# Starting the first FFN block in halves, separate PSUM tiles for the q and k transposes, and x of two groups transposed by DMA, in a fused chunk-attention and FFN kernel

## The chip, the cores and the metric

The kernel runs on one core of a Trainium2 chip. TensorE multiplies matrices and writes to PSUM tiles; VectorE, ScalarE and GpSimd copy, cast and work element by element; SyncE issues DMA transfers. The granted clock is the share of TensorE's full speed that the profile shows as granted: 1.00 is full, 0.50 is half. The metric is the device time of one execution in microseconds (us). Most executions of one kernel agree within a per cent or so; a run that is over 1.5% above the fastest of the same kernel on its chip is called slow and is left out of comparisons. Ratios below are the mean time of one kernel's fast runs over the mean of the other's fast runs in the same rounds on the same chip, so they are not quite the ratio of the medians that are quoted beside them. The kernel before alone had medians of 298 to 301 us on the chips used here, so times from different chips are not compared to less than a per cent.

## The reference, cut to what matters

```python
# q, k, v: (8 batches, 8 heads, 576 positions, 64), float32; attention inside chunks of 64 positions
scores = scale * q_c @ k_c.T            # per chunk
attn   = softmax(scores)
x      = (attn @ v_c) -> (4608 tokens, 512)
out    = relu(x @ w_in)**2 @ w_out      # w_in (512, 2048), w_out (2048, 512)
```

The 4,608 tokens are 18 groups of 256. Two groups make an FFN block of 512 tokens, nine blocks in all (0 to 8).

## The kernel before

TensorE runs the FFN of one block while the attention of the next block is slipped in between, at numbered slots: one slot per `ft` (one of 16 column tiles of `w_in`) of the first FFN matmul, then one per quarter of an output tile of the second. For groups 0 to 3, q and k are transposed on TensorE; from group 4 on they are loaded, cast to bf16 by GpSimd (`C`) and transposed by DMA (`TD`). x is transposed on TensorE below group `FIRST_DMA_X` and by DMA from there on. SyncE issues the loads and the transposes in program order; where an instruction waits, those behind it wait too.

```python
FIRST_DMA_T = 4
FIRST_DMA_X = 6
ps_ffn = tile_pool(name="ps_ffn", bufs=4, PSUM)      # tiles of 128 x 512 fp32
ps_att = tile_pool(name="ps_att", bufs=2, PSUM)      # tiles of 128 x 1024 fp32

def transpose_qk(g):
    ps = ps_att.tile([128, 1024], FP32, name="ps_att").bitcast(BF16)   # q and k in one tile
    ...
    for which in range(2):
        transpose_paired(g, which, ps[:, which * 1024:(which + 1) * 1024])
    for which, copy in enumerate((nc.vector.tensor_copy, nc.scalar.copy)):
        copy_paired(copy, qkT[:, which], ps[:, which * 1024:(which + 1) * 1024])

# ... the start: filler matmuls (keep_busy) between the pieces of the first attention
XE(0); keep_busy(8); AV(1); keep_busy(8)
transpose_x_early(1, 0); keep_busy(4); transpose_x_early(1, 1); keep_busy(4)

# ... the plan by slots; SC = scores, AV = values, XT = transpose of x
if j == 0:
    for slot, f in ((24, T), (27, SC), (29, AV), (31, XT)):
        at(slot, f, nxt[0])
    at(31, T, nxt[1])
    phases = [ffn_in(0, 0, 512), ffn_out_by_ft(0)]
elif j == 1:
    go_slots = [*range(17), *range(34, 48)]           # one load issued in each of these slots
    loads = itertools.chain(pieces(nxt), *map(qk_pieces, far))
    ...
    for i, g in enumerate(nxt):
        for slot, f in ((22 + 4 * i, C), (27 + 4 * i, TD), (37, SC), (39 + 2 * i, AV), (42 + 2 * i, XT)):
            at(slot, f, g)
else:
    slots = {SC: 8, AV: 11, XT: 15, C: 14, TD: 19}
    if j == 2:
        slots = {SC: 6, AV: 11, XT: 14, C: 20, TD: 24}
    ...
# at the end of block 1: C and TD of groups 6 and 7
```

In block 1 `nxt` is groups 4 and 5 and `far` is groups 6 and 7. The loads of q and k of 6 and 7 go out in slots 34 to 43, their casts and transposes at the end of the block, and their scores stand in slot 6 of block 2.

The softmax here doesn't subtract the row's maximum and nothing guards it: scores larger than these inputs give would overflow.

## Time and profile before

| | before |
|---|---|
| median of the first three runs | 298.04 us (296.81 to 302.14) |
| profiled execution | span 294.9 us, granted clock 1.00 |
| TensorE busy | 282.1 us, 96% |
| start of the first FFN matmul of block 1 / second of block 1 / first of block 2 / first of block 3 | 52.60 / 70.27 / 86.86 / 116.28 us |

The main lines of this profile stand in the prediction below. Four more are SyncE's issues of the last loads and transposes ahead of block 2's scores (start, duration, line, what):

```profile
77.55 0.83 SPq L110 DMA_DIRECT2D k_sb<-in_k_dram  x1
...
80.44 2.97 SPq L110 DMA_DIRECT2D q_sb<-in_q_dram  x1
83.46 0.91 SPq L110 DMA_DIRECT2D k_sb<-in_k_dram  x1
84.55 6.57 SPq L223 DMA_TRANSPOSE qkT<-qkb  x2
```

The two transposes of q and k follow the last load. The second of them lands at 93.3 us (issued 89.40, 3.9 us), where the scores of groups 6 and 7 run (93.06 to 93.76).

### The profile page before, as it was taken

How to read it: one execution, taken by the hardware profiler on the slowest of the kernel's cores; microseconds unless marked ns; L12 is line 12 of the kernel's file. 1: busy time of each engine (PE TensorE's matmuls, PEld its weight loads, DVE VectorE, ACT ScalarE, POOL GpSimd, SP SyncE). 2: the span in 40 equal slices, each digit the busy share in tenths (PEclk: the TensorE clock that was granted, in tenths of full speed). 3: DMA queues.
4: the chain of work that ended last, by engine and by line, in shares of the span. 5: the costliest groups of instructions: out<-in, count | busy, mean ns of one | idle time of the engine just before them, and what ended most of it. 6: DMA issues, size and time to landing. Idle time of an engine off the chain costs nothing.

```text
span 294.9 us, 6372 instructions
## 1 busy us (share of the span) xinstructions
PE 282.1 (96%) x2590; PEld 142.5 (48%) x2590; DVE 114.1 (39%) x247; ACT 129.8 (44%) x225; POOL 48.7 (17%) x68
## 2 busy tenths in 40 slices
PE   2899999899999999999999999999999999999995
PEld 1684444776454444444444444444444444444442
DVE  1347903695234720562046205720672056205400
ACT  1427505655428612771177117712771277127511
POOL 2046840050041022022004102300310000000000
PEclk9999999999999999999999999999999999999999
DMA  7999999999998999999999999899977501320011
GB/s 203 242 338 362 385 272 224 256 209 184 251 229 215 210 212 223 239 196 207 237 238 207 190 235 253 183 201 255 242 137 144 160 36 33 76 81 29 0 71 71
DMA packets 158381, 57.04 MB, mean 193 GB/s; under 512 B 139280, under 2 KB 151824, under 8 KB 158352
## 3 DMA queue, kind: packets, MB, share of 16 engines
q1 hardware_dynamic: 152640, 46.81, 76.6%
q10 hardware_dynamic: 5712, 9.83, 9.9%
q8 instruction: 20, 0.33, 0.5%
q14 instruction: 9, 0.07, 0.1%
HBM read 36.70 MB, written 9.44 MB: 156 GB/s over the span
## 4 chain that ended last, share of the span: by engine, by line
PE 88%; DMA 5%; SPq 4%; ACT 1%; issue 1%; DVE 0%
PE ps_ffn L312 40%; PE ps_ffn L328 35%; PE ps_ffn L357 5%; PE ps_att L260 3%; PE ps_att L237 2%; DMA out_dram<-o_sb 2%; DMA vo_sb<-in_v_dram 2%; DMA qkT<-qkb 1%; SPq L102 1%; SPq L117 1%; PE ps_ffn L210 1%; SPq L223 1%; SPq L124 1%; PE ps_att L287 1%; PE ps_att L164 1%
## 5 line engine op out<-in xcount | busy, mean ns | idle before, releaser
L312 PE MATMUL ps_ffn<-xT,w_in_bf 128*128 128x512 bf16 (+1 forms) x640 | 129.0, 358 | 2.0 <-ACT rl L318 1.5
L319 DVE TENSOR_TENSOR gT<-rl 128x512 bf16<-128x512 bf16 (+1 forms) x160 | 76.2, 492 | 128.7 <-ACT rl L318 126.2
L328 PE MATMUL ps_ffn<-w_out_bf,gT 128*128 128x512 bf16 x512 | 112.7, 379 | 0.0
L318 ACT ACTIVATE rl<-ps_ffn 128x512 bf16<-128x512 f32 (+1 forms) x160 | 86.2, 558 | 38.4 <-PE ps_ffn L312 34.9
L312 PEld LDWEIGHTS <-w_in_bf 128*128 128x128 bf16 x640 | 61.2, 98 | 62.1 <-issue 1.4
L328 PEld LDWEIGHTS <-gT 128*128 128x128 bf16 x512 | 49.3, 98 | 58.0
L345 ACT COPY o_sb<-ps_ffn 128x512 f32<-128x512 f32 x31 | 18.1, 585 | 91.3 <-PE ps_ffn L328 85.4
L216 POOL CAST qkb<-q_sb 128x1024 bf16<-128x1024 f32 x14 | 14.7, 1048 | 139.5 <-DMA q_sb<-in_q_dram 120.3
L268 DVE TENSOR_TENSOR x<-ps_att,rec 128x512 bf16<-128x512 f32 x36 | 24.9, 691 | 1.2
L244 ACT ACTIVATE e<-ps_att 128x1024 bf16<-128x1024 f32 x18 | 17.6, 1024 | 4.7 <-PE ps_att L237 4.7
L216 POOL CAST qkb<-k_sb 128x1024 bf16<-128x1024 f32 x14 | 15.4, 1099 | 6.5 <-DMA k_sb<-in_k_dram 4.8
L357 PE MATMUL ps_ffn<-w_out_bf,gT 128*128 128x512 bf16 x64 | 14.7, 379 | 0.0
L267 DVE RECIPROCAL rec<-ps_att 128x8 f32<-128x8 f32 x36 | 7.2, 199 | 13.5 <-PE ps_att L260 13.5
L139 POOL CAST w_in_bf<-w_st 128x1024 bf16<-128x1024 f32 (+1 forms) x9 | 8.5, 956 | 19.1 <-DMA w_st<-in_moe_w_in_dram 19.1
L260 PEld LDWEIGHTS <-e 64*64 64x64 bf16 x576 | 7.0, 111 | 8.5 <-ACT rl L318 2.3
L260 PE MATMUL ps_att<-vo_sb,e 64*64 64x65 bf16 x288 | 9.2, 201 | 1.2 <-DMA vo_sb<-in_v_dram 1.0
L357 PEld LDWEIGHTS <-gT 128*128 128x128 bf16 x64 | 6.0, 97 | 7.2 <-DVE gT L319 0.3
L147 POOL CAST w_out_bf<-w_st 128x1024 bf16<-128x1024 f32 x8 | 8.8, 1098 | 2.1 <-DMA w_st<-in_moe_w_out_dram 2.1
L260 PE MATMUL ps_att<-ve_sb,e 64*64 64x65 bf16 x288 | 9.1, 201 | 0.0
L237 PEld LDWEIGHTS <-qkT 64*64 64x64 bf16 x576 | 6.1, 112 | 4.4 <-issue 3.0
L237 PE MATMUL ps_att<-qkT 64*64 64x64 bf16 x576 | 7.6, 200 | 0.3 <-DMA qkT<-qkb 0.3
L173 ACT COPY qkT<-ps_att 128x512 bf16<-128x512 bf16 x4 | 2.1, 588 | 11.9 <-DVE qkT L173 9.8
(31 smaller groups left out, 49.2 us busy)
## 6 DMA issues: line engine op xcount, KB each, us to landing
out_dram<-o_sb ACTq DMA_DIRECT2D x35, 256.0 KB, 3.5
q_sb<-in_q_dram SPq DMA_DIRECT2D x25, 256.0 KB, 5.0
k_sb<-in_k_dram SPq DMA_DIRECT2D x25, 256.0 KB, 5.2
ve_sb<-in_v_dram SPq DMA_DIRECT2D x32, 128.0 KB, 4.1
vo_sb<-in_v_dram SPq DMA_DIRECT2D x32, 128.0 KB, 3.9
w_st<-in_moe_w_out_dram SPq DMA_DIRECT2D x8, 512.0 KB, 5.7
w_st<-in_moe_w_in_dram SPq DMA_DIRECT2D x7, 512.0 KB, 7.0
q_sb<-in_q_dram SPq DMA_DIRECT2D x3, 512.0 KB, 6.7
```

What stands on the lines that cost most here:

```text
L147: nc.gpsimd.tensor_copy(out=w_out_bf[:, 2 * i:2 * i + 2, :], in_=st)
L216: nc.gpsimd.tensor_copy(out=qkb[:, which], in_=qk[g][which].rearrange("p t h d -> p (t h d)"))
L237: nc.tensor.matmul(out=ps[64 * c:64 * c + 64, o0:o0 + 64], lhsT=qkT[64 * a:64 * a + 64, 1, t, hp, cols], rhs=qkT[64 * a:64 * a + 64, 0, t, ...
L244: nc.scalar.activation(out=e.rearrange("p a h t q -> p (a h t q)"), in_=ps, func=AF.Exp, scale=scale)
L260: nc.tensor.matmul(out=ps[64 * p:64 * p + 64, a, hp * (D + 1):(hp + 1) * (D + 1)], lhsT=e[64 * c:64 * c + 64, a, hp, t, :], rhs=vb[64 * c: ...
L268: nc.vector.tensor_tensor(out=x[:, t].rearrange("p h a d -> p a h d"), in0=o[:, :, :, 0:D], in1=rec.to_broadcast([128, 2, n_hp, D]), op=AL ...
L312: nc.tensor.matmul(out=h[:, 0:n], lhsT=w_in_bf[:, dt, ft * 128:(ft + 1) * 128], rhs=xT[:, c // 128:(c + n) // 128, dt, :], start=(dt == 0) ...
L318: nc.scalar.activation(out=rl[:, 0:n], in_=h[:, 0:n], func=AF.Relu)
L319: nc.vector.tensor_tensor(out=gT[:, ft, c:c + n], in0=rl[:, 0:n], in1=rl[:, 0:n], op=ALU.mult)
L328: nc.tensor.matmul(out=o_ps, lhsT=gT[:, ft, tt * 128:(tt + 1) * 128], rhs=w_out_bf[:, ft, :], start=(ft == 0), stop=(ft == n_ft - 1))
L345: nc.scalar.copy(out=o_sb, in_=o_ps)
L357: nc.tensor.matmul(out=o_ps[tt], lhsT=gT[:, ft, tt * 128:(tt + 1) * 128], rhs=w_out_bf[:, ft, :], start=(ft == 0), stop=(ft == n_ft - 1))
```

## The change

The intent is to use TensorE's time better in three places. The filler at the start gives way to real FFN work: the first four `ft` run for group 0 alone and later for group 1. The q and k transposes get a PSUM tile each, so that VectorE and ScalarE can copy them side by side. The 16 TensorE transposes of x for groups 4 and 5 become two DMA transposes, which SyncE issues between the loads; the loads make room for them (slots 34 to 38, then 44 to 47).

```diff
-    FIRST_DMA_X = 6
+    FIRST_DMA_X = 4
...
+    def transpose_qk(g, q_pool, k_pool):
...
+        for which, pool in enumerate((q_pool, k_pool)):
+            copy = nc.scalar.copy if which else nc.vector.tensor_copy
+            (bank = a tile of that pool)
             transpose_paired(g, which, bank)
             copy_paired(copy, qkT[:, which], bank)
...
     XE(0)
-    keep_busy(8)
     AV(1)
-    keep_busy(8)
+    n_early = 4
+    early = ffn_in(0, [(0, 256, range(n_early)), (256, 256, range(n_early)),
+                       (0, 512, range(n_early, n_ft))])
+    next(early)
     transpose_x_early(1, 0)
-    keep_busy(4)
+    next(early)
     transpose_x_early(1, 1)
-    keep_busy(4)
...
-            for slot, f in ((24, T), (27, SC), (29, AV), (31, XT)):
+            for slot, f in ((26, TA), (29, SC), (31, AV), (33, XT)):
-            at(31, T, nxt[1])
+            at(33, TM, nxt[1])
...
-            go_slots = [*range(17), *range(34, 48)]
+            go_slots = [*range(17), *range(34, 39), *range(44, 48)]
-            for slot, f in ((4, SC), (8, AV), (12, XT)):
+            for slot, f in ((4, SC), (7, AV), (12, XT)):
-                                (42 + 2 * i, XT)):
+                                (41 + 2 * i, XT)):
...
-            slots = {SC: 8, AV: 11, XT: 15, C: 14, TD: 19}
+            slots = {SC: 9 if j == 3 else 8, AV: 11, XT: 15, C: 14, TD: 19}
```

`TA` puts both tiles in the attention pool, `TM` puts k in the FFN pool.

More of the change, by code (lines that the diff above doesn't have):

```diff
@@ L173, in copy_paired @@
             copy(out=dst[:, t], in_=src[:, t])
-    def transpose_qk(g):
-        ps = ps_att.tile([128, 1024], FP32, name="ps_att").bitcast(BF16)
+    def transpose_qk(g, q_pool, k_pool):
         qkT = att_pool.tile([128, 2, 2, n_hp, 128], BF16, name="qkT", bufs=4)
         state["qkT", g] = qkT
-        for which in range(2):
-            transpose_paired(g, which, ps[:, which * 1024:(which + 1) * 1024])
-        for which, copy in enumerate((nc.vector.tensor_copy, nc.scalar.copy)):
-            copy_paired(copy, qkT[:, which], ps[:, which * 1024:(which + 1) * 1024])
-    def transpose_qk_early(g, k_copy):
-        qkT = att_pool.tile([128, 2, 2, n_hp, 128], BF16, name="qkT", bufs=4)
-        state["qkT", g] = qkT
-        for which, copy in enumerate((nc.vector.tensor_copy, k_copy)):
-            bank = ps_ffn.tile([128, 512], FP32, name="ps_ffn").bitcast(BF16)
+        for which, pool in enumerate((q_pool, k_pool)):
+            copy = nc.scalar.copy if which else nc.vector.tensor_copy
+            if pool is ps_ffn:
+                bank = pool.tile([128, 512], FP32, name="ps_ffn")
+            else:
+                bank = pool.tile([128, 1024], FP32, name="ps_att")
+            bank = bank.bitcast(BF16)[:, 0:1024]
             transpose_paired(g, which, bank)
@@ L291, in transpose_x, with TA, TM @@
         nc.vector.tensor_copy(out=dst, in_=psb)
-    T, C, TD = transpose_qk, cast_qk, transpose_qk_dma
+    C, TD = cast_qk, transpose_qk_dma
     SC, AV, XT = scores, values, transpose_x
+    def TA(g):
+        transpose_qk(g, ps_att, ps_att)
     def TE(g):
-        transpose_qk_early(g, nc.scalar.copy)
+        transpose_qk(g, ps_ffn, ps_ffn)
+    def TM(g):
+        transpose_qk(g, ps_att, ps_ffn)
     def XE(g):
@@ L303, with ffn_in @@
     gTs = {}
-    def ffn_in(j, c, n):
+    def ffn_in(j, parts):
         if j not in gTs:
@@ L308, in ffn_in @@
         gT, xT = gTs[j], xTs[j]
-        for ft in range(n_ft):
+        for c, n, ft in ((c, n, ft) for c, n, fts in parts for ft in fts):
             h = ps_ffn.tile([128, 512], FP32, name="ps_ffn")
@@ L382 @@
     go(pieces([0, 1]))
-    transpose_qk_early(0, nc.scalar.copy)
+    TE(0)
     keep_busy(8)
@@ L386 @@
     keep_busy(6)
-    transpose_qk_early(1, nc.scalar.copy)
+    TE(1)
     load_w_in(0, nc.scalar, 2)
@@ L417 @@
             loads, go_slots = iter(()), []
-            for slot, f in ((24, T), (27, SC), (29, AV), (31, XT)):
+            for slot, f in ((26, TA), (29, SC), (31, AV), (33, XT)):
                 at(slot, f, nxt[0])
-            at(31, T, nxt[1])
-            phases = [ffn_in(0, 0, 512), ffn_out_by_ft(0)]
+            at(33, TM, nxt[1])
+            phases = [early, ffn_out_by_ft(0)]
         elif j == 1:
-            go_slots = [*range(17), *range(34, 48)]
+            go_slots = [*range(17), *range(34, 39), *range(44, 48)]
             loads = itertools.chain(pieces(nxt), *map(qk_pieces, far))
-            for slot, f in ((4, SC), (8, AV), (12, XT)):
+            for slot, f in ((4, SC), (7, AV), (12, XT)):
                 at(slot, f, grps[1])
@@ L428 @@
                 for slot, f in ((22 + 4 * i, C), (27 + 4 * i, TD), (37, SC), (39 + 2 * i, AV),
-                                (42 + 2 * i, XT)):
+                                (41 + 2 * i, XT)):
                     at(slot, f, g)
-            phases = [ffn_in(1, 0, 256), ffn_in(1, 256, 256), ffn_out(1)]
+            phases = [ffn_in(1, [(0, 256, range(n_ft)), (256, 256, range(n_ft))]), ffn_out(1)]
         else:
             loads, go_slots = pieces(far), range(32)
-            slots = {SC: 8, AV: 11, XT: 15, C: 14, TD: 19}
+            slots = {SC: 9 if j == 3 else 8, AV: 11, XT: 15, C: 14, TD: 19}
             if j == 2:
@@ L444 @@
                 at(slots[TD] + 3 * i, TD, g)
-            phases = [ffn_in(j, 0, len(grps) * GT), ffn_out(j)]
+            phases = [ffn_in(j, [(0, BT, range(n_ft))]), ffn_out(j)]
         slot = 0
```

## The prediction

> **What bounds the kernel now.** I read the page first, then the chain of waits in order of time, then the timeline of three stretches, then single loads by tile and window.
>
> ```profile
> span 294.9 us, 6372 instructions
> ...
> PE 282.1 (96%) x2590; PEld 142.5 (48%) x2590; DVE 114.1 (39%) x247; ACT 129.8 (44%) x225; POOL 48.7 (17%) x68
> ...
> DMA  7999999999998999999999999899977501320011
> ...
> PE 88%; DMA 5%; SPq 4%; ACT 1%; issue 1%; DVE 0%
> ```
>
> TensorE is busy 96% of the span, so there are only 294.9 - 282.1 = 12.8 us without a matmul, and 6.7 us of that lie in the first 14 us (7.33 us busy there in the view by windows), before the loads are in, and 3.5 us after the last matmul at 291.4. But the row of DMA digits is as full as TensorE's until about 220 us. So TensorE cannot simply be moved forward: whatever waits for a load of q, k or v is pinned to the arrival of that load. The chain of waits shows both faces:
>
> ```profile
> 14.27 0.43 PE ps_att L260 x13
> ...
> 18.54 0.97 PE ps_ffn L210 x8
> ...
> 19.93 0.35 PE ps_ffn L210 x4
> ...
> 20.29 0.24 PE ps_ffn L199 x4
> 21.12 13.97 PE ps_ffn L312 x64
> ...
> 54.10 1.06 ACT qkT L173 x2
> ...
> 62.65 0.40 ACT rl L318
> ...
> 81.67 0.58 PE ps_att L287 x8
> ...
> 83.98 0.45 PE ps_att L287 x8
> ...
> 93.06 0.70 PE ps_att L237 x64
> ...
> 116.98 2.96 SPq L223
> ...
> 120.65 4.20 DMA qkT<-qkb
> ...
> 124.90 0.45 PE ps_att L237 x32
> ```
>
> L210 is filler work, L199 and L287 are transposes of x, L312 is the first FFN matmul, L237 the scores. At 54.1 and 62.7 us TensorE waits for ScalarE; at 124.9 it waits for a DMA transpose of q and k. The timeline shows why ScalarE is late at 54 us:
>
> ```profile
> 52.72 1.29 DVE L173 COPY qkT<-ps_att 128x512 bf16<-128x512 bf16 x2 [0.33 <-PE ps_att L164]
> ...
> 54.09 1.07 ACT L173 COPY qkT<-ps_att 128x512 bf16<-128x512 bf16 x2 [2.12 <-PE ps_ffn L312]
> ...
> 55.50 0.60 PE L312 MATMUL ps_ffn<-xT,w_in_bf 128*128 128x256 bf16 x4 [0.98 <-ACT rl L318]
> ```
>
> The k transposes end near 52.7, but the k copy starts when VectorE's q copy ends (54.01): the two halves of one PSUM tile are read one after the other. The four FFN tiles of PSUM fill meanwhile and TensorE stands 0.98 us.
>
> **What the Trainium skill says.** "TensorE: Matmul & The Clock Gate", section "Back-to-back issue gap", gives N/2.4 + 2.5 ns: 216 ns at 512 columns, 109 at 256. The trace agrees roughly: 13.97/64 = 218 ns, and the chain's 36 half-width matmuls in 4.10 us are 114 ns. So halves cost 8 x 4 x 114 = 3.65 us in place of 16 x 218 = 3.49. "PSUM — Partial Sum Buffer", section "PSUM bank collisions raise a hardware error", says that two engines must not be on one bank and quadrant at once, reads included, so accesses have to be ordered. Here q and k lie in separate banks already (1,024 bf16 are 2 KiB each), yet the trace shows the order; the guard seems to be kept by tile, and tiles of their own should lift it. "DMA: Bandwidth & Descriptors", section "Issuing engines are not separate DMA queues", says that all transfers end on the same 16 engines and interleave, and its section "Latency and other measured facts" puts the DMA transpose at 261 GB/s, 1.0 us for 0.26 MB. A transpose by DMA is therefore not free where the DMA row is full; no trace shows its rate by itself.
>
> **The change, part by part.**
>
> *The start.* Of the filler, 8 + 8 + 4 + 4 matmuls go; the halves of group 0's first FFN tiles go into their place. The weights limit it. The casts of w_in (POOL) run at 17.58 (two of 0.6 us, for ft 0 and 1), 19.63, 21.14 and then every 1.5 us, each 1.04 long. Values of group 1 cannot end earlier: the last odd v, issued at 11.88, landed 6.2 us later, at 18.1. So: ft 0 at 18.5, the transposes of x between, ft 1 by 19.9, then ft 2 waits for the cast that ends at 20.67. From there six halves, 6 x 0.457 = 2.74, give ft 4 at 23.4. Before, ft 4 stands at 21.12 + 4 x 0.873 = 24.6. Offered: 1.2 us. Later casts (22.2 for ft 4, 23.7 for ft 6, 29.8 for ft 14) remain ahead of TensorE.
>
> How much is kept? The schedule moves group 3's transposes by the two added slots only, so they come at 43.06 - 1.2 = 41.9, their k half at 42.3. The k of group 3, issued at 35.0, took 8.2 us to land: 43.2, and in the kernel before its half starts at 43.46. So about 0.9 us turns into a wait for k. Kept: 0.3 us.
>
> *The PSUM tiles.* At 54 us the 0.98 us wait should go, since the k copy can start at 52.4. With values one slot earlier, the 0.5 us wait near 62.5 (VectorE behind with the products of x) should go for the most part. Offered: 1.3 us. But the scores of groups 4 and 5 stand at 75.61 to 76.26, and their q and k come by DMA transpose; the second is issued at 70.83 and takes 4.9 us: 75.7. The stream in front of it is paced by the DMA, which does not get shorter. I keep 0.2 to 0.5 us in all at this place, 0.4 as the middle.
>
> *x of groups 4 and 5 by DMA.* This lies after that pin. It removes L287's 0.58 + 0.45 = 1.03 us of TensorE and two copies of 0.69 us on VectorE, which is idle there. TensorE could start block 2 at 87.02 - 0.4 - 1.03 = 85.6. VectorE writes the second x of group 5 from 81.72 to 82.41, now 82.0; existing x transposes take 3.1 to 6.0 us to landing, median 4.0, so it lands at 85.1 to 88, middle 86.0: a wait of about 0.4, and TensorE is 1.0 us ahead.
>
> The price: both transposes move 2 x 0.262 MB, at the 225 GB/s measured between 70.44 and 87.02 us that is 2.3 us of a full DMA. They also stand in SyncE's in-order queue, which has to wait for x, ahead of five loads of q and k of groups 6 and 7. Before, the last of these (issued 83.46, 4.8 us) lands at 88.3; its cast ends at 89.4; the transpose takes 3.9 us: 93.3, exactly where the scores of 6 and 7 stand (93.06 to 93.76). With 1.0 to 2.3 us more it lands at 94.3 to 95.6, while TensorE arrives at 86.0 + 6.04 = 92.0. This is a new wait of 2.3 to 3.6 us, and with 0.35 us for the second scores TensorE would leave that point at 94.65 to 95.95, 0.9 to 2.2 us later than before.
>
> *Block 3* puts the scores of groups 8 and 9 one slot (0.87 us) later, which takes up the 0.3 us wait at 124.9 and up to 0.6 us of a later stream. It adds no work. From about 146 us on transposes of q and k land well ahead of their scores, so nothing is won or lost.
>
> Sum with full DMA cost: +0.9 to +2.2, less 0.3: about +1.2 us. Sum if the extra DMA work is absorbed: -1.0 - 0.3 = -1.3, perhaps -1.8.
>
> **The rivals.** (1) The DMA queue becomes the bound between 80 and 95 us: new waits of the first scores in block 2 for the q and k transpose. For it: the DMA digits of 9, and the exact fit of 93.3 against 93.06. Time +0.5 to +2. (2) The DMA absorbs the two transposes, since the loads of v behind them are spread and the DMA's share between 84 and 92 us is only 0.98 to 1.04 against up to 1.2 elsewhere; and whoever moved block 3's scores a slot back left those of block 2 at slot 6. Then TensorE's saving stays: -1.3 to -2. (3) All offers are kept, 1.2 + 1.3 + 1.0 + 0.3 = 3.8 us: it needs loads that run earlier because TensorE does. Some waits of SyncE are for output transfers, so part of the stream does follow TensorE; against it stand the pinned arrivals at 43.2 and 75.7. (4) The clock falls because filler is gone. The new gaps on TensorE are 0.4 us at most, and the granted clock is 9 in all slices; I give it 2%.
>
> **Range and chances.** I give rival 1 a little over half, rival 2 a third, rival 3 a tenth: 0.55 x 1.2 - 0.35 x 1.5 - 0.1 x 3.8 = -0.2 us. The three times before are 296.81, 298.04 and 302.14, so the noise of a median is about 1 us and larger than this; from 298.04 I predict 297.8 us, and a range of 294.6 to 300.8. A gain of 2% needs 6 us, more than everything offered; a loss of 2% would need the wait at the scores of block 2 to repeat in several blocks. Chances: faster 0.02, within 2% 0.95, slower 0.03.
>
> **What would show it.** Right or wrong can be read by step: ft 4 of the first block near 23.4 us instead of 24.6; a wait of TensorE for k_sb near 42.3; no wait of ScalarE's k copy for VectorE at L173, and no 0.98 us wait after it; scores of groups 4 and 5 at about 75 us with a wait for the q and k transpose; block 2's first matmul about 86 us, behind a wait for xT; and the largest new row, scores waiting 2.3 to 3.6 us for the q and k transpose in 92 to 96 us. If that last row is absent, rival 2 holds and the kernel is 1 to 2 us faster; if the scores of groups 4 and 5 are also over 1 us earlier, the loads follow TensorE and rival 3 holds. A slower result of over 2% would show waits on DMA in blocks 3 to 5 too.

## The result, and the profile after

The changed kernel took 306.83 us (median of 4 runs, 304.92 to 307.30), beside 300.09 us for the kernel before (4 runs, 296.81 to 303.04). The ratio of the fast runs is 1.0304, 95% interval 1.0218 to 1.0390: slower by 3%. The prediction was 297.8 us with a range up to 300.8, and gave "slower by over 2%" a chance of 3%. It was wrong.

Two cautions. Of the four runs of the kernel before, 302.14 and 303.04 lie over 1.5% above the fastest and are left out, so this ratio rests on two runs; two later measurements of the same pair, on other chips, gave 1.0255 and 1.0171 (below). And the profiled execution of the kernel before was one of its fastest (296.72 us): the two profiles are 10.6 us apart, the means of the fast runs 9.0, 7.2 and 6.0 us in the three measurements. The profiles say where the time went in one execution, not how much on average.

The page of the changed kernel, the same rows as before, with the row of the granted clock:

```profile
span 305.5 us, 6323 instructions
...
PE 282.9 (93%) x2546; PEld 142.5 (47%) x2566; DVE 116.8 (38%) x249; ACT 131.7 (43%) x229; POOL 49.9 (16%) x68
...
PEclk9959999999599599999999999999999999999999
DMA  7999999999899899999799999969994800410011
...
PE 84%; DMA 7%; SPq 5%; issue 1%; DVE 1%; ACT 0%; POOL 0%; POOLq 0%
```

TensorE has the same busy time as before, but the span is 10.6 us longer, DMA has a larger share of the chain that ended last, and three slices ran at half the clock (the first of them in the start). Who TensorE waited for (us in total, times, longest):

```profile
PE ps_att L233 <- DMA qkT<-qkb: 7.6, 4, 3.1
...
PE ps_att L256 <- DMA vo_sb<-in_v_dram: 2.8, 4, 1.4
PE ps_ffn L314 <- DMA xT<-x: 1.0, 1, 1.0
```

The scores (L233 now, L237 before) wait 7.6 us for q and k transposed by DMA, where they waited 0.3 before; this is their row on the page before:

```profile
L237 PE MATMUL ps_att<-qkT 64*64 64x64 bf16 x576 | 7.6, 200 | 0.3 <-DMA qkT<-qkb 0.3
```

The starts of the four stages, read from the timelines, say where the 10.6 us arose:

| stretch | before | after | difference |
|---|---|---|---|
| block 1, first FFN matmul (from 52.60 / 52.63) | 17.67 | 15.59 | -2.08 |
| block 1, second FFN matmul (from 70.27 / 68.22) | 16.59 | 22.87 | +6.28 |
| block 2 (from 86.86 / 91.09) | 29.42 | 36.24 | +6.82 |
| block 3 to the end (from 116.28 / 127.33) | 178.62 | 178.17 | -0.45 |

So the first part of the change had won nothing by 52.6 us, the second part then won 2.1 us, and two stretches lost 13.1 us. In both of these the timeline has the same pattern (the bracket is TensorE's idle time before the row):

```profile
74.25 0.45 PE L233 MATMUL ps_att<-qkT 64*64 64x64 bf16 x32 [0.69 <-DMA qkT<-qkb]
...
77.26 0.64 PE L233 MATMUL ps_att<-qkT 64*64 64x64 bf16 x32 [2.56 <-DMA qkT<-qkb]
...
78.23 3.19 PE L330 MATMUL ps_ffn<-w_out_bf,gT 128*128 128x512 bf16 x7 [0.33 <-issue]
...
98.50 0.44 PE L233 MATMUL ps_att<-qkT 64*64 64x64 bf16 x32 [1.20 <-DMA qkT<-qkb]
...
102.05 0.64 PE L233 MATMUL ps_att<-qkT 64*64 64x64 bf16 x32 [3.11 <-DMA qkT<-qkb]
```

TensorE waits for q and k of one group, then of the next, and afterwards its matmuls are slow: the 7 of 512 columns in 3.19 us start 0.43 us apart, against 0.22 in the kernel before. (The 0.33 us of "issue" ahead of them is no wait: eight weight loads stand there beside seven matmuls, so one matmul's record is missing. The page counts 495 matmuls of this line and 512 weight loads.) The view by windows shows it as the granted clock (columns: stretch, its length, busy time and instructions of PE, PEld, DVE, ACT and POOL, granted clock, DMA share, GB/s), first in the changed kernel, then in the kernel before:

```profile
76.20:83.00 6.80, 5.41 (x74) 2.50 (x76) 1.06 (x4) 1.61 (x2) 1.04 (x1) 0.50 0.87 149
...
100.20:106.90 6.70, 4.85 (x43) 2.04 (x44) 0.44 (x2) 2.22 (x3) 0.00 (x0) 0.50 0.81 181
```

```profile
76.20:83.00 6.80, 6.80 (x105) 3.29 (x98) 3.99 (x9) 2.38 (x3) 1.51 (x2) 1.00 1.22 265
100.20:106.90 6.70, 6.70 (x62) 3.10 (x61) 3.85 (x10) 2.38 (x4) 2.08 (x2) 1.00 1.36 208
```

Why q and k came late is in SyncE's queue, the same stretch as shown of before:

```profile
77.69 0.63 SPq L110 DMA_DIRECT2D q_sb<-in_q_dram  x1
83.78 3.96 SPq L277 DMA_TRANSPOSE xT<-x  x2
87.79 1.19 SPq L110 DMA_DIRECT2D k_sb<-in_k_dram  x1
...
90.36 1.05 SPq L110 DMA_DIRECT2D q_sb<-in_q_dram  x1
91.47 1.39 SPq L110 DMA_DIRECT2D k_sb<-in_k_dram  x1
93.02 6.52 SPq L219 DMA_TRANSPOSE qkT<-qkb  x2
```

Between 78.3 and 83.8 us SyncE issues nothing: it stands at the first transpose of x, whose x is not written yet (VectorE's last product of group 4 ran from 82.95 to 83.64), and the five loads of groups 6 and 7 stand behind it. The last of them goes out at 91.47 instead of 83.46.

The theory after this reading, W: TensorE runs ahead of the DMA stream, stands at the scores of groups 5 and 7, and the clock falls after each stand; the DMA transposes of x hold up the stream itself. Rivals: the DMA transposes alone do the harm and being ahead is free (R); and, inside the DMA part, the cost is in the order of the queue, or in the bytes.

### The profile page after: what moved, and what is told of

The parts are those of the page before. It is cut to its first block, busy times and chain, and to the rows that moved or that the text cites.

```text
span 305.5 us, 6323 instructions
## 1 busy us (share of the span) xinstructions
PE 282.9 (93%) x2546; PEld 142.5 (47%) x2566; DVE 116.8 (38%) x249; ACT 131.7 (43%) x229; POOL 49.9 (16%) x68
## 3 DMA queue, kind: packets, MB, share of 16 engines
q1 hardware_dynamic: 154752, 47.33, 76.2%
## 4 chain that ended last, share of the span: by engine, by line
PE 84%; DMA 7%; SPq 5%; issue 1%; DVE 1%; ACT 0%; POOL 0%; POOLq 0%
PE ps_ffn L314 40%; PE ps_ffn L330 35%; PE ps_ffn L359 5%; DMA qkT<-qkb 3%; PE ps_att L256 2%; DMA vo_sb<-in_v_dram 2%; DMA q_sb<-in_q_dram 2%; PE ps_att L233 2%; SPq L117 1%; SPq L102 1%; SPq L124 1%; SPq L219 1%; PE ps_att L164 1%; DVE gT L321 0%; POOL qkb L212 0%
## 5 line engine op out<-in xcount | busy, mean ns | idle before, releaser
L314 PE MATMUL ps_ffn<-xT,w_in_bf 128*128 128x512 bf16 (+1 forms) x656 | 132.5, 359 | 1.4 <-DMA xT<-x 1.0
L321 DVE TENSOR_TENSOR gT<-rl 128x512 bf16<-128x512 bf16 (+1 forms) x164 | 80.3, 507 | 133.7 <-ACT rl L320 131.2
L330 PE MATMUL ps_ffn<-w_out_bf,gT 128*128 128x512 bf16 x495 | 113.2, 384 | 1.3 <-issue 0.5
L320 ACT ACTIVATE rl<-ps_ffn 128x512 bf16<-128x512 f32 (+1 forms) x164 | 87.6, 547 | 43.1 <-PE ps_ffn L314 37.5
L314 PEld LDWEIGHTS <-w_in_bf 128*128 128x128 bf16 x656 | 63.5, 99 | 62.0 <-issue 2.7
L330 PEld LDWEIGHTS <-gT 128*128 128x128 bf16 x512 | 49.8, 99 | 59.9 <-issue 1.9
L212 POOL CAST qkb<-k_sb 128x1024 bf16<-128x1024 f32 x14 | 16.3, 1161 | 11.0 <-DMA k_sb<-in_k_dram 10.8
L233 PE MATMUL ps_att<-qkT 64*64 64x64 bf16 x576 | 8.0, 203 | 7.6 <-DMA qkT<-qkb 7.6
L233 PEld LDWEIGHTS <-qkT 64*64 64x64 bf16 x576 | 6.4, 115 | 11.8 <-DMA qkT<-qkb 8.8
L256 PEld LDWEIGHTS <-e 64*64 64x64 bf16 x576 | 7.0, 112 | 10.6 <-DMA vo_sb<-in_v_dram 3.7
L164 PE MATMUL ps_ffn<-ident,q_sb 128*64 128x128 bf16 x32 | 2.1, 313 | 4.9 <-DMA q_sb<-in_q_dram 4.9
```

The lines of the kernel that those rows point to most:

```text
L212: nc.gpsimd.tensor_copy(out=qkb[:, which], in_=qk[g][which].rearrange("p t h d -> p (t h d)"))
L233: nc.tensor.matmul(out=ps[64 * c:64 * c + 64, o0:o0 + 64], lhsT=qkT[64 * a:64 * a + 64, 1, t, hp, cols], rhs=qkT[64 * a:64 * a + 64, 0, t, ...
L256: nc.tensor.matmul(out=ps[64 * p:64 * p + 64, a, hp * (D + 1):(hp + 1) * (D + 1)], lhsT=e[64 * c:64 * c + 64, a, hp, t, :], rhs=vb[64 * c: ...
L314: nc.tensor.matmul(out=h[:, 0:n], lhsT=w_in_bf[:, dt, ft * 128:(ft + 1) * 128], rhs=xT[:, c // 128:(c + n) // 128, dt, :], start=(dt == 0) ...
L320: nc.scalar.activation(out=rl[:, 0:n], in_=h[:, 0:n], func=AF.Relu)
L321: nc.vector.tensor_tensor(out=gT[:, ft, c:c + n], in0=rl[:, 0:n], in1=rl[:, 0:n], op=ALU.mult)
```

## The experiments

All 15 runs gave correct results.

### One part alone, or without

`no_dma_x` is the changed kernel with the third part undone:

```diff
-    FIRST_DMA_X = 4
+    FIRST_DMA_X = 6
-            go_slots = [*range(17), *range(34, 39), *range(44, 48)]
+            go_slots = [*range(17), *range(34, 48)]
-                                (41 + 2 * i, XT)):
+                                (42 + 2 * i, XT)):
```

> The changed kernel with x of groups 4 and 5 transposed on TensorE again. Theory W (TensorE runs ahead of the DMA stream, stands over 2 us at the scores of groups 5 and 7, and its clock then falls to half for 6.8 us): one wait of 2 to 2.5 us for the q and k transpose of group 5 near 75 us stays and with it one stretch of half clock, but the loads of groups 6 and 7 are no longer held up, so the second wait shrinks; 298 to 301 us, 5 to 8 us under the changed kernel. Rival R (the DMA transposes alone do the harm, being ahead is free): 294 to 296 us.

Measured: 300.04 us beside 298.95, ratio 1.0015 (0.9984 to 1.0045). The median lies in W's range and R falls: all of the gain of the first two parts is gone. Its trace has one wait of 2.6 us for the q and k of group 5 and a granted clock of 0.79 over the 8 us from 76 to 84.

`dma_x_alone` is the kernel before with the third part only (the same three lines, the other way round).

> The kernel before with only the third part: x of groups 4 and 5 by DMA and the loads behind them. W: no wait at the scores of groups 4 and 5 since TensorE is not ahead, a wait under 1.5 us for x at the start of block 2, 2 to 4 us for the q and k of group 7, and half clock after that one: 299 to 303 us. R: the same 303 us or more as the whole change less its gain, that is 305 to 308 us.

Measured: 304.05 us beside 298.95, ratio 1.0152 (1.0088 to 1.0215). The median lies 1 us above W's range and 1 us below R's; by ratio to its own chip's kernel before it is half of the whole loss, which W said and R did not. The profiled execution was a slow one, so only the ratio is used. (W expected no wait at the scores of groups 4 and 5; that slow trace has one of 2.1 us there. The landing that these scores need moves between executions, as shown further down.)

`tiles_alone` is the kernel before with the q and k transposes in two tiles, and `halves_alone` the kernel before with the early halves and the slots of block 0 moved by two:

```diff
# tiles_alone
-            for slot, f in ((24, T), (27, SC), (29, AV), (31, XT)):
+            for slot, f in ((24, TA), (27, SC), (29, AV), (31, XT)):
-            at(31, T, nxt[1])
+            at(31, TM, nxt[1])
# halves_alone
     XE(0)
-    keep_busy(8)
     AV(1)
-    keep_busy(8)
+    early = ffn_in(0, [(0, 256, range(4)), (256, 256, range(4)), (0, 512, range(4, n_ft))])
+    next(early)
     transpose_x_early(1, 0)
-    keep_busy(4)
+    next(early)
     transpose_x_early(1, 1)
-    keep_busy(4)
```

> The kernel before with only the PSUM tiles of q and k apart. W: the wait of 0.98 us for ScalarE goes, TensorE reaches the scores of groups 4 and 5 1 us earlier and waits about 1 us there, under what drops the clock: within 0.5% of before. R: the gain of 1 us is kept, 296 us or less beside a before of 297.

> The kernel before with only the first four ft in halves. In the changed kernel the first FFN block ended at 35.08 us, before at 35.09, so nothing was won there: within 0.5% of before under W and R. If the half clock that its trace shows from 14.8 to 21.6 us is due to the removed filler and costs time, it would be 1 to 2 us slower.

Measured: `tiles_alone` 299.44 us, ratio 1.0038 (1.0012 to 1.0064); `halves_alone` 298.81 us, ratio 0.9974 (0.9947 to 1.0001), both beside 298.95. In `tiles_alone` the wait for ScalarE is gone, but the scores wait 2.9 us for q and k, the longest 2.2, and the clock is at 0.79 from 76 to 84 us: the gain turned into a wait and a little more. R expected a kept gain and falls. W has the time right (within 0.5%), but it expected a wait of about 1 us and no fall of the clock, and missed both. The halves win a quarter of a per cent, with an interval from half a per cent to nothing. Their clock was 0.50 from 14 to 21 us, and they are no slower than the kernel before: the slow clock at the start costs nothing that these runs can see.

The parts do not add up: 0.26% faster, 0.38% slower and 1.5% slower would be 1.6% slower, and the whole was 3.0%. That would fit being ahead and being late adding up at the same scores, but it is not firm: the changed kernel was measured at 1.017 and 1.026 of before in later rounds, and 1.017 would be the sum of the parts.

### Queue order or bytes

`loads_first` puts all ten loads of groups 6 and 7 ahead of the two transposes of x:

```diff
-            go_slots = [*range(17), *range(34, 39), *range(44, 48)]
+            go_slots = [*range(17), *range(32, 42)]
```

> The changed kernel with all ten loads of q and k of groups 6 and 7 ahead of the two transposes of x in SyncE's queue. Theory order (the loads are late because the queue stands for x, not for the bytes of the transposes): k of group 7 lands by 90 us instead of 96.6 and its q and k transpose by 96 instead of 102.0; the x of group 5 lands 1 to 3 us later in place; 301 to 304 us. Theory bytes (the two transposes take DMA time): k of group 7 lands at 88 to 91 but the rest of the stream is as late as before, 305 to 307 us.

Measured: 302.66 us beside 301.11, ratio 1.0049 (1.0020 to 1.0077). Most of the loss is gone, with the same transposes. The last k of group 7 is issued at 82.98 and lands 6.2 us later, at 89.2, not at 96.6. TensorE now waits 2.6 us for x at the start of block 2, as expected, and 3.0 us for q and k. The range of the order theory (301 to 304 us) is met. So the place in the queue matters:

```profile
82.98 1.55 SPq L110 DMA_DIRECT2D k_sb<-in_k_dram  x1
84.64 4.80 SPq L277 DMA_TRANSPOSE xT<-x  x2
```

This run does not separate the stand for x from the transposes' own time, since both now come behind the loads. (The profiled execution counts as slow, so these figures of its trace are pointers.)

`extra_transposes` is the kernel before with two DMA transposes of 256 KB added in the middle of those loads, of an x that is ready since long ago, into tiles that nobody reads:

```diff
+    scratch = [w_pool.tile([128, 8, 128], BF16, name=f"scratch{i}") for i in range(2)]
+    def EX(g):
+        nc.sync.dma_start_transpose(
+            out=scratch.pop(), in_=state["last_x"].rearrange("p t h a d -> p (t h a d)"))
...
+            at(38, EX, 2)
+            at(39, EX, 2)
             phases = [ffn_in(1, 0, 256), ffn_in(1, 256, 256), ffn_out(1)]
```

> The kernel before with two DMA transposes of the same size added at the same place, of x of group 2 that is long ready, into tiles that nobody reads. Theory order: only their own DMA time shows, the q and k of group 7 land 1 to 2.5 us later and the kernel is 0 to 2 us slower than before (under 0.7%). Theory bytes: as the third part alone, 1.5% slower.

Measured: 304.98 us beside 301.11, ratio 1.0157 (1.0091 to 1.0222). The pure order theory expected under 0.7% and falls: 0.5 MB of transposes that wait for nothing cost as much as the third part alone, as the theory of the bytes expected. So both count: a transfer's own time, and the stand of the queue.

`extra_loads` has two plain loads of the same 256 KB in the same place instead:

```diff
-        nc.sync.dma_start_transpose(out=scratch.pop(), in_=...)
+        nc.sync.dma_start(out=scratch.pop(), in_=q[2, :, 0:128, :].rearrange("h s d -> s h d"))
```

> The kernel before with two plain loads of 256 KB each, in pieces of 256 B, at the place in the queue where the run of extra transposes had two transposes of 256 KB. Theory T (a transpose by DMA costs more of the stream than its bytes, about 2 us each in the trace of the extra transposes, against 1.2 from the mean rate): k of group 7 lands about 2.5 us later than before instead of 4 to 6, the ratio is under 1.010 and clearly below the 1.016 of the transposes. Theory B (bytes are bytes): 1.012 to 1.018.

Measured: 303.88 us beside 300.17, ratio 1.0145 (1.0086 to 1.0204). That is what "bytes are bytes" expected, and in time a transpose is not told apart from a load. The traces do differ somewhat. Counted from the first of the ten loads, the last q of group 7 lands 12.5 us later in the kernel before (issued 73.68; the last one issued at 80.44 and 5.8 us to landing), 15.4 with the extra loads (74.07; 85.31 and 4.2) and 16.9 with the extra transposes (75.43; 86.93 and 5.4). Two extra loads delay it by 2.9 us, two extra transposes by 4.4. So theory T was about right on the landing (2.5 us) and wrong on the ratio.

The profile of this run is the clearest of all, since one thing makes up nearly the whole of its loss (timeline, then windows):

```profile
93.51 0.45 PE L237 MATMUL ps_att<-qkT 64*64 64x64 bf16 x32
98.23 0.45 PE L237 MATMUL ps_att<-qkT 64*64 64x64 bf16 x32 [4.27 <-DMA qkT<-qkb]
98.60 4.64 PE L318 MATMUL ps_ffn<-xT,w_in_bf 128*128 128x512 bf16 x13
```

```profile
98.60:102.00 3.40, 3.40 (x20) 1.19 (x10) 0.42 (x1) 1.62 (x2) 0.00 (x0) 0.50 1.15 213
```

One wait of 4.27 us and then 3.4 us at half clock, in which half of the work, 1.7 us, is lost: 6.0 us, and the span is 301.1 - 294.9 = 6.2 us longer than that of the kernel before.

`extra_late` moves two such transposes to block 5, where the DMA row of the page is as full. They were issued at 203.1 and 204.4 us, not near 197 as expected: behind that block's own transposes of q and k, and ahead of loads for a later block.

```diff
-            at(38, EX, 2)
-            at(39, EX, 2)
...
             loads, go_slots = pieces(far), range(32)
+            if j == 5:
+                at(24, EX, 2)
+                at(25, EX, 2)
```

> The kernel before with the two extra transposes moved to block 5, near 197 us, where the DMA is as full but the q and k transposes land 5 to 9 us ahead of their scores. Theory slack (extra DMA work costs only where the scores stand right behind the landing): within 0.3% of before. Rival (every us of DMA work is a us of the span): 1.010 or more.

Measured: 300.31 us beside 300.17, ratio 0.9998 (0.9965 to 1.0032). The same work costs nothing there. So a busy DMA alone does not make such work cost time (its share between 190 and 206 us is 1.19 in the kernel before, and 1.12 between 76 and 84); what differs is the slack between a landing and its use.

### The clock

`fill_waits` puts filler matmuls into the waits of the changed kernel, so that TensorE does not stand:

```diff
# block 1, slot 37:  scores of 4, keep_busy(40), scores of 5
# block 2, slot 6:   keep_busy(15), scores of 6, keep_busy(50), scores of 7
+    def KB(g):
+        keep_busy(40)
+                if j == 2:
+                    at(slots[SC], lambda g, n=50 if i else 15: keep_busy(n), g)
                 at(slots[SC], SC, g)
```

> The changed kernel with idle-time filler: 40 small matmuls of the identity between the scores of groups 4 and 5, 15 ahead of those of group 6 and 50 between those of 6 and 7, in the waits of 2.6, 1.2 and 3.1 us that its trace shows. Theory W with its second half (the clock falls because TensorE stood, and the slow matmuls cost 2 to 3 us each time and delay x of groups 4 and 5, so the loads behind it): no half clock at 76 and 100 us, values of group 4 some 2 us earlier, 300 to 303 us against 305 to 307 for the changed kernel. Rival (the waits cost, the clock is a side effect): 305 to 308 us, filler being work.

Measured: 303.70 us beside 301.11, ratio 1.0132 (1.0050 to 1.0214), and a granted clock of 1.00 in the whole of the profiled execution (0.981 to 0.989 in the other three, of which no trace was kept). The median lies between the two expectations, 0.7 us above W's range and 1.3 below the rival's. That was on another chip than the changed kernel. So the changed kernel was run again, twice, the second time beside the filler version with five rounds, and with the same filler in the third part alone:

> The changed kernel unaltered, as the same-chip reference for the other three: 1.025 to 1.035 of the kernel before, as in the first measurement (1.030).

> The changed kernel, as the reference on this chip: 1.025 to 1.031 of before.

> The changed kernel with filler in the waits, again. If the half clock costs time of its own (waits alike, clock full): 1.010 to 1.018 of before, at least 1 point under the changed kernel beside it. If the clock is only a side effect: within 0.5 points of the changed kernel.

> The third part alone, with the same filler. Alone it was 1.015. Theory: the later landing of group 7's q and k stays, some 3 to 5 us of wait at its scores less the slack, and the clock loss of about 2 us goes: 1.006 to 1.012. If the clock costs nothing here: 1.015 again.

| run | median | before beside it | ratio, 95% interval |
|---|---|---|---|
| `after_again` | 306.90 | 300.17 | 1.0255 (1.0185 to 1.0325) |
| `after_third` | 306.40 | 301.28 | 1.0171 (1.0122 to 1.0219) |
| `fill_again` | 304.88 | 301.28 | 1.0127 (1.0098 to 1.0157) |
| `dma_x_fill` | 306.38 | 301.28 | 1.0147 (1.0105 to 1.0190) |

The changed kernel itself is steady, 306.4 to 306.9 us three times; it is the kernel before that was slower on the last chip. `after_third` (1.0171) missed its expectation of 1.025 to 1.031. Side by side the filler gains 1.5 us in the medians and 0.44 points in the ratio, and the intervals overlap. Its theory of the clock had asked for at least 1 point and missed; the rival's "within 0.5 points" is met. `dma_x_fill` too gave what was expected if the clock costs nothing: 1.0147 with the filler, where the third part alone had 1.0152 on another chip.

The list of all runs says a little more than the medians. On the last chip the fast runs of the changed kernel have a mean time of 306.7 us and a mean clock of 0.981, those of the filler version 304.6 and 0.990, those of the kernel before 300.7 and 0.991. The filler brings the clock back to that of the kernel before, and 2.1 us of 6.0 (by the ratios 0.44 points of 1.71) come back with it: a quarter to a third of the loss. This is one chip, and the filler is itself work. In the single trace the clock's part is 5.3 us (worked out below), but that execution, at 0.966, has nearly the lowest clock of the 14 runs of the changed kernel (0.965 to 0.989), and the executions differ: the trace of `after_third` has half clock after the second stand (103.5 to 106.9 us) and none after the first, though its first stand, 0.70 and 2.53 us, is like that of the changed kernel's first trace. What the filler runs do show is that most of the loss stays when the clock is as in the kernel before: the wait itself is the larger part.

### A version that beats both

`spread_no_dma_x` was the first try: no DMA for x of groups 4 and 5, and the scores moved behind the point where their data lands.

```diff
 # on top of no_dma_x
-  block 1:  (37, SC), (39 + 2 * i, AV), (42 + 2 * i, XT)
+  block 1:  (37 + 4 * i, SC), (39 + 5 * i, AV), (42 + 4 * i, XT)
-  block 2:  SC 6 and 6, AV 11 and 15, XT 14 and 17
+  block 2:  SC 9 and 13, AV 12 and 17, XT 16 and 20
-  later:    SC 8 and 8 (9 in block 3), AV 11 and 15, XT 15 and 18
+  later:    SC 10 and 12, AV 12 and 16, XT 16 and 20
```

> The changed kernel with x of groups 4 and 5 on TensorE again and the scores moved behind where their data lands: group 5 from slot 37 to 41, groups 6 and 7 from slot 6 to 9 and 13, later ones from 8 or 9 to 10 and 12. Theory W: TensorE fills the waits with FFN matmuls, no wait over 1 us for q and k and no half clock after 25 us, and the 2 us won in block 1 are kept: 294 to 296 us, 1% under the kernel before. Rival (the DMA stream sets the end, whatever the slots): 298 to 300 us.

Measured: 311.60 us beside 301.11, ratio 1.0286 (1.0181 to 1.0391). Two of its four runs are slow ones and in the median; the ratio uses the other two. This was an error of the schedule, not an answer:

```profile
PE ps_att L233 <- DVE rec L263: 8.8, 5, 2.1
```

In the later blocks the second scores stood in slot 12 right behind the first values. They take the PSUM tile that VectorE has not yet read, and TensorE waited 1.8 us on average, five times. In blocks 1 and 2 the idea worked: only 0.8 us of waits for q and k are left.

`spread2` keeps the later blocks as in the changed kernel and moves less in block 2:

```diff
 # on top of no_dma_x
-  block 1:  (37, SC), (39 + 2 * i, AV), (42 + 2 * i, XT)
+  block 1:  (37 + 4 * i, SC), (39 + 5 * i, AV), (42 + 4 * i, XT)
-  block 2:  SC 6 and 6, AV 11 and 15, XT 14 and 17
+  block 2:  SC 8 and 10, AV 12 and 15, XT 15 and 17
```

> A version meant to beat both: halves and PSUM tiles kept, x of groups 4 and 5 on TensorE, the scores of group 5 four slots later and those of groups 6 and 7 two and four slots later, later blocks as in the changed kernel. The first try at this lost 2 us in every block because the second scores stood behind the values of the same slot; that is undone. If W is right: no q and k wait over 1 us in blocks 1 and 2, no half clock after 25 us, 0.990 to 0.998 of before. Rival (DMA stream sets the end): 0.998 to 1.003.

Measured: 297.87 us beside 300.17, ratio 0.9931 (0.9904 to 0.9958): 0.7% faster than the kernel before, and about 3% faster than the changed one. The chain of waits of its block 1 and 2 shows scores that no longer wait:

```profile
74.95 0.38 PE ps_att L233 x32
...
79.39 0.38 PE ps_att L233 x32
...
94.29 0.38 PE ps_att L233 x32
94.67 1.83 PE ps_ffn L314 x8
96.50 0.37 PE ps_att L233 x32
```

FFN matmuls (L330, L314) stand where the waits were, and the clock is full from 25 us to the last matmul. The 1.2 us for q and k that its list of waits still has lie in block 3. W's signs and range are met. One rival is untested: no run moves the scores in the kernel before alone. Its scores wait 0.3 us in the profile, so little would be expected of that.

## Why the prediction was wrong

**The start.** Offered 1.2 us, kept 0.3. Measured: nothing. Full-width work (ft 4) began near 24.6 us, 22.80 plus four halves of 0.44, as before. (`halves_alone` leaves at most half a per cent.) The prediction had the casts of the weights as the limit. In fact the second x copy of VectorE came at 22.3 to 22.7 us, behind a product of the early halves, and the first halves ran at half clock:

```profile
18.74 1.03 PE L314 MATMUL ps_ffn<-xT,w_in_bf 128*128 128x256 bf16 x4
...
22.33 0.41 DVE L200 COPY xT<-ps_ffn 128x512 bf16<-128x512 bf16 x1
...
22.80 2.57 PE L314 MATMUL ps_ffn<-xT,w_in_bf 128*128 128x256 bf16 x19 [0.32 <-DVE xT L200]
```

The first row is 1.03 us for four halves where 0.46 was taken; the clock of 14.8 to 21.6 us was 0.50. The forecast wait for k at 42.3 us did not come, since TensorE was not early.

**The PSUM tiles.** Right in kind and larger than said: the k copy no longer waits for the q copy (it ran from 52.74, VectorE's from 52.28), the 0.98 us wait is gone, and the stretch became 2.08 us shorter where 1.3 was offered.

**The pin at groups 4 and 5.** This step said that a gain beyond 0.4 us would turn into a wait there and cost nothing else. The q and k of group 5 landed at 77.2 (issued 72.30, 4.9 us), not at 75.7; TensorE stood 0.69 + 2.56 us, and the clock fell. The prediction took 75.7 from one trace as fixed. It moves: in `extra_late` and `extra_transposes`, which equal the kernel before up to there, the landing is at 76.1 and 77.5 us. `tiles_alone` and `no_dma_x` show that this alone eats the gain of 2 us.

**The price of the DMA transposes.** The mechanism was named: rival 1, the scores of group 7 behind a late transpose, and its signs came (a wait for x at the start of block 2, 1.03 us; waits of 1.20 and 3.11 us for q and k in block 2). This is the term of the sum that was mis-sized most: q and k of group 7 were to land 1.0 to 2.3 us later, at 94.3 to 95.6, and landed at 102.0 (98.23 and 3.8), 8.7 us later. Over the fast runs the third part alone costs 1.5%, about 4.5 us. The 2.3 us are the bytes at the mean rate of 225 GB/s; how the low end of 1.0 arises is not said. Measured, from the start of the ten loads to the landing of the last q: 12.5 us before, 21.3 in the changed kernel (74.57 to 95.87), a delay of 8.8 us (by the last k, 14.5 and 22.1: 7.6 us). About 4.4 of that is what two transposes that wait for nothing cost (`extra_transposes`). The rest fits the stand of SyncE at x, which the prediction mentioned ("has to wait for x") and gave no time; `loads_first`, which takes the stand away and the transposes' own time with it, lands that q 11.9 us after the first load (75.44; 81.64 and 5.7), no later than before. x itself was late in this trace because the scores of group 5 and the matmuls behind them were, so the first stand fed the second.

**The clock.** This step failed outright: no time was set down for it. Rival 4 had 2%, on the ground that "the new gaps on TensorE are 0.4 us at most", while the same text forecast a wait of 2.3 to 3.6 us at the scores of group 7. Every forecast wait ought to have been put to the question what the clock does after it. In the trace of the changed kernel the clock is 0.50 from 76.2 to 83.0 and from 100.1 to 106.9 us, and TensorE works there from 77.26 and from 102.05 on; half of that time is lost, 2.9 and 2.4 us. The pieces give the same: in block 1 16 matmuls (one without a record) in 3.5 + 2.4 us where 16 x 0.218 = 3.5 were due, 2.4 us, and some 0.4 in the scores and values; in block 2 20 matmuls in 6.54 us where 4.4 were due, 2.2 us, and 0.3 in the scores. With the waits, block 1 has 0.69 + 2.56 + 1.03 + 2.8 less the 1.03 of removed transposes = 6.1 us against +6.28 measured; block 2 has 1.20 + 3.11 + 2.5 = 6.8 against +6.82. So 5.3 us of that execution are clock and 8.6 us are waits. On average the clock's part is smaller: by the filler runs a quarter to a third of the loss, 1.3 to 2.1 us, on one chip and with overlapping intervals.

**Range and chances.** "Slower" was tied to a wait that repeats in several blocks. Two blocks were enough, and the sign it gave for a slower result, waits on DMA in blocks 3 to 5, stayed away: from block 3 to the end the changed kernel is 0.45 us shorter.

What the runs leave is this: the schedule before had the landing of q and k of groups 5 and 7 (75.7 and 93.3 us) and the scores that use them within 0.2 us of each other. Work taken off TensorE ahead of such a place becomes a wait; DMA work added ahead of it becomes a wait as well; the change did both, and in one of them put the loads behind an instruction that itself waited for TensorE. Moving the scores to where their data is, with the third part undone (`spread2`), made a kernel with the first two parts 0.7% faster than the one before.

## What to carry to other kernels

Before you take work off a busy engine, find the next place where it meets data from a stream that is full, and compare landing and use there: if they touch, the saving is a wait unless the use moves too. Before you add a transfer to an in-order queue, count three things and not only its bytes: its own time, how long the queue will stand at it for its input, and the slack of the first transfer behind it. And when a wait of 2 us or more on TensorE comes out of a forecast, add the slow clock that may follow: here falls followed stands of 2.0 to 4.3 us, though not every one.

## What the Trainium skill lacked or had wrong

- "TensorE: Matmul & The Clock Gate", section "Why this matters for your kernels", gives the rule that idle gaps over about 3 us between bursts of matmuls take the clock back to half. Here shorter stands did: 2.6 us in `no_dma_x`, 0.7 and 2.2 close together in `tiles_alone`, 0.69 and 2.56 in the changed kernel. With each of these the clock went to 0.50 for 3.4 or 6.8 us (a mean of 0.79 over 8 us is 3.4 us at half). It is not a threshold either: 0.70 and 2.53 us in the trace of `after_third` brought no fall.
- The same page, section "Back-to-back issue gap", gives about 131 ns per matmul of 512 columns as a sustained rate in a real kernel; here 64 in a row took 13.97 us, 218 ns each, close to the section's isolated figure (about 216).
- "DMA: Bandwidth & Descriptors", section "Latency and other measured facts", gives 261 GB/s for the DMA transpose (non-contiguous case), from which 256 KB are an estimate of 1.0 us, and no figure beside other traffic. Beside a full stream of 256-byte loads two such transposes delayed what was behind them by 4.4 us, 2.2 each, and two plain loads of the same size by 2.9 us.
- No page gives a figure for what a DMA in an in-order issuing queue costs the transfers behind it when its input is late. Here the queue stood for 5.5 us. The two orders were 1.2 to 2.5 points of ratio apart, in different rounds (1.0171 to 1.0304 with the loads behind, 1.0049 with them ahead); part of that is the transposes' own time.
